# RWKV-6 attention with a SwiGLU layer: two of four batches of superblocks 2 and 3 get their normed x transposed by DMA

## Chip, cores and metric

The kernel runs on one core of one Trainium2 chip. The metric is the device time of one execution in microseconds (us). Its median before the change is 200.54 us, of 3 runs from 200.46 to 200.59.

## What is computed

The first part is an attention with a state (RWKV-6), over 4 batches, 8 heads, 768 time steps and a head size of 48. The second is a feed-forward layer (SwiGLU) over the 3072 rows that result, each 8 x 48 = 384 wide:

```
for t in range(S):                                  # each batch b, head h
    cur   = (u * k[t]) outer v[t]
    y[t]  = r[t] @ (state + cur)
    state = w[t][:, None] * state + k[t] outer v[t]

x  = y as (3072, 384)
xn = x / sqrt(mean(x*x) + 1e-6) * rms_g
out = (silu(xn @ w_gate) * (xn @ w_val)) @ w_out    # 384 -> 1536 -> 384
```

The change concerns the line of `xn`: x of a row divided by its root mean square, times the weights rms_g of the norm, and brought into the layout that the products with w_gate and w_val read.

## The kernel before

Time is cut into 6 superblocks (n) of 128 steps. Within one, each of the 4 batches (j) goes through the attention on its own, with 128 steps on the partitions and all 8 heads side by side (128x384). Then the feed-forward layer of the superblock runs over the 512 rows of its 4 batches at once: 12 blocks (f) of 128 columns of w_gate and w_val, and last the product with w_out, batch by batch.

All steps stand in one list, ORDER, as `function.n.j` (or `function.n.f`), and a loop at the end of the kernel calls them in that order. What an engine does is in the order of that list; an engine that waits holds back all that is behind it on that engine. SP issues nearly all DMAs from one queue, in order, and each waits there for its inputs and for an earlier transfer to have landed. The attention of superblock n+1 is mixed into the feed-forward steps of superblock n.

From the output y of a batch to the products, the steps are:

- `x_add` (L561, DVE), `x_sq` (L570, ACT) and `x_rstd` (L579 and L580, POOL) make x and one over its root mean square.
- `xn_mul` (L585, ACT) writes xn, 128x384 in bf16, still without rms_g.
- In superblocks 0 to 3, `xn_pe` (L596, PE) transposes it in three 128x128 pieces into a PSUM bank, and `xn_out` (L607, DVE) multiplies that by the weights gT, 128x384 at once, into the tile xnt (128 x 3 x 512: rms_g's index on the partitions, KC = 3 chunks of 128, and 128 columns for each batch).
- In superblocks 4 and 5, `xn_tr` (L590) lets a DMA transpose xn straight into xnt, and `xn_gain` (L615, on DVE, one chunk on ACT) multiplies xnt in place, a chunk of 128x512 for all four batches at a time.
- `gate_mm` and `val_mm` (L626, PE) read all 512 columns of xnt, so the first of a superblock waits for the last batch.

Other lines that are spoken of: L672 is `o_mm`, the product with w_out (PE). L425 is `cs_add`, L455 `r_mul`, L451 `w_tot`, L472 `bonus_sum` and L679 `o_out` (all DVE). L461 is `k_mul`, from superblock 2 on POOL, and L467 and L468 are the two products of `bonus_mul` (POOL), the second of which reads what the first wrote. L489 is `rk_tr`, the DMA transpose of r and k that `q_mm` (L502 and L504, PE) reads. L248 and L261 are the loads.

Of the kernel before, what the change touches and what calls it, by code (L numbers as in the profile page):

```python
# [74 lines left out]
exp_k.3.3 cs_mm.3.2 xn_out.2.3 o_mm.1.2 load_r.3.2 k_mul.3.1 w_tot.3.3 rk_tr.3.0 r_mul.3.3 cs_add.3.2 out_dma.1.0
xn_out.2.1 load_v.3.0 exp_r.3.2 gate_mm.2.5 exp_k.3.2 r_mul.3.2 w_tot.3.2 val_mm.2.0 gate_mm.2.0 bonus_mul.3.0
bonus_mul.3.2 k_mul.3.2 o_out.1.3 bonus_sum.3.0 silu.2.5 rk_tr.3.1 load_k.3.3 o_out.1.2 q_mm.3.0 silu.2.0 q_mask_e.3.0
val_mm.2.1 bonus_v.3.0 h_mul.2.0 gate_mm.2.1 load_w.4.1 load_v.3.1 load_k.4.3 st_mm.3.2 k_mul.3.3 q_copy_o.3.0
silu.2.1 rk_tr.3.2 load_v.4.0 rk_tr.3.3 val_mm.2.5 gate_mm.2.11 load_k.4.0 bonus_sum.3.1 cast_v.3.0 out_dma.1.1
load_v.3.3 load_w.5.2 q_mask_e.3.1 q_copy_o.3.1 gate_mm.2.2 silu.2.11 h_mul.2.5 val_mm.2.2 h_mul.2.1 load_w.4.0  # L80
gate_mm.2.3 load_v.4.1 silu.2.2 q_mask_o.3.0 cast_v.3.1 load_r.4.1 bonus_sum.3.2 h_mul.2.2 bonus_v.3.1 gate_mm.2.6
val_mm.2.3 y_mm.3.0 st_new.3.2 st_mm.3.0 silu.2.3 gate_mm.2.4 h_mul.2.3 silu.2.6 q_mask_o.3.1 st_new.3.0 st_mm.3.1
silu.2.4 x_add.3.0 load_k.4.1 gate_mm.2.7 val_mm.2.4 x_sq.3.0 gate_mm.2.10 out_dma.1.2 cast_v.4.0 st_new.3.1
val_mm.2.6 q_mm.3.2 h_mul.2.4 bonus_mul.3.3 h_mul.2.6 silu.2.7 val_mm.2.7 val_mm.2.10 load_w.4.3 x_rstd.3.0 silu.2.10
# [5 lines left out]
o_out.2.0 x_rstd.3.2 xn_mul.3.2 w_tot.4.0 ln.4.2 exp_r.4.1 load_r.5.1 x_rstd.3.3 k_mul.4.0 xn_out.3.0 load_r.4.3  # L90
out_dma.1.3 bonus_sum.4.1 xn_pe.3.1 xn_out.3.1 ln.4.3 exp_k.4.1 bonus_mul.4.2 xn_mul.3.3 r_mul.4.1 k_mul.4.1 w_tot.4.1
out_dma.2.0 o_mm.2.1 cs_mm.4.2 xn_pe.3.3 bonus_mul.4.0 cast_v.4.1 xn_pe.3.2 o_out.2.1 cs_mm.4.3 bonus_sum.4.2
rk_tr.4.0 xn_out.3.3 cs_add.4.3 load_k.5.3 o_mm.2.3 exp_r.4.3 xn_out.3.2 cs_add.4.2 bonus_mul.4.3 r_mul.4.3 w_tot.4.3
exp_k.4.3 exp_r.4.2 rk_tr.4.1 o_out.2.3 exp_k.4.2 load_v.4.2 val_mm.3.1 gate_mm.3.6 bonus_sum.4.0 k_mul.4.3 r_mul.4.2
st_mm.4.0 w_tot.4.2 load_r.5.3 load_k.5.0 val_mm.3.0 o_out.2.2 silu.3.6 st_new.4.0 k_mul.4.2 gate_mm.3.1 q_mm.4.0
cast_v.4.2 out_dma.2.2 bonus_sum.4.3 silu.3.1 gate_mm.3.0 q_copy_o.4.0 silu.3.0 h_mul.3.1 q_copy_o.4.1 gate_mm.3.3
val_mm.3.6 gate_mm.3.8 rk_tr.4.3 q_mask_e.4.0 h_mul.3.0 h_mul.3.6 st_mm.4.1 bonus_v.4.0 q_mask_e.4.1 q_mask_o.4.0
load_r.5.0 bonus_v.4.2 rk_tr.4.2 load_v.5.1 q_mask_o.4.1 bonus_v.4.1 silu.3.3 gate_mm.3.4 val_mm.3.4 val_mm.3.3
y_mm.4.0 silu.3.4 st_new.4.1 gate_mm.3.9 h_mul.3.4 load_v.4.3 load_r.5.2 load_k.5.1 silu.3.8 x_add.4.0 val_mm.3.8
gate_mm.3.2 q_mm.4.2 h_mul.3.3 h_mul.3.8 silu.3.9 val_mm.3.9 load_w.5.1 silu.3.2 gate_mm.3.10 q_mask_e.4.3  # L100
q_copy_o.4.3 y_mm.4.1 h_mul.3.9 bonus_mul.5.3 x_sq.4.0 q_mask_o.4.3 x_rstd.4.0 q_copy_o.4.2 bonus_v.4.3 silu.3.10
x_add.4.1 load_w.5.3 val_mm.3.10 gate_mm.3.7 q_mask_e.4.2 x_sq.4.1 bonus_sum.5.3 xn_mul.4.0 load_w.5.0 x_rstd.4.1
h_mul.3.10 silu.3.7 val_mm.3.2 gate_mm.3.5 h_mul.3.2 load_k.5.2 gate_mm.3.11 q_mask_o.4.2 y_mm.4.2 cast_v.4.3
xn_mul.4.1 val_mm.3.7 silu.3.5 bonus_mul.5.0 x_add.4.2 silu.3.11 ln.5.1 y_mm.4.3 h_mul.3.7 val_mm.3.11 x_add.4.3
load_v.5.3 x_sq.4.2 xn_tr.4.0 h_mul.3.11 x_sq.4.3 xn_tr.4.1 val_mm.3.5 st_mm.4.3 h_mul.3.5 x_rstd.4.2 cs_mm.5.1
cs_add.5.1 ln.5.2 xn_mul.4.2 x_rstd.4.3 o_mm.3.2 o_out.3.2 cs_mm.5.2 xn_tr.4.2 exp_k.5.1 cs_add.5.2 exp_r.5.1 o_mm.3.0
xn_mul.4.3 r_mul.5.1 ln.5.3 ln.5.0 xn_tr.4.3 cs_mm.5.0 st_new.4.3 exp_r.5.2 cast_v.5.3 exp_k.5.2 o_mm.3.1 out_dma.3.2
cs_add.5.0 out_dma.2.3 r_mul.5.2 exp_r.5.0 cs_mm.5.3 r_mul.5.0 st_mm.4.2 exp_k.5.0 cs_add.5.3 exp_r.5.3 o_mm.3.3
bonus_mul.5.1 xn_gain.4.0 xn_gain.4.2 xn_gain.4.1 k_mul.5.0 r_mul.5.3 exp_k.5.3 o_out.3.1 out_dma.2.1 o_out.3.0
gate_mm.4.0 val_mm.4.1 gate_mm.4.1 val_mm.4.0 bonus_sum.5.1 st_new.4.2 k_mul.5.1 k_mul.5.3 silu.4.0 load_v.5.0  # L110
rk_tr.5.0 silu.4.1 h_mul.4.0 gate_mm.4.3 gate_mm.4.2 rk_tr.5.1 silu.4.3 val_mm.4.2 bonus_sum.5.0 k_mul.5.2 gate_mm.4.4
silu.4.2 bonus_v.5.1 o_out.3.3 cast_v.5.0 h_mul.4.1 val_mm.4.3 q_mm.5.0 gate_mm.4.6 h_mul.4.2 bonus_mul.5.2 h_mul.4.3
silu.4.4 q_copy_o.5.0 q_mask_o.5.0 gate_mm.4.5 out_dma.3.1 q_mask_e.5.0 y_mm.5.0 silu.4.6 q_copy_o.5.1 bonus_v.5.0
rk_tr.5.2 load_v.5.2 silu.4.5 rk_tr.5.3 x_add.5.0 val_mm.4.4 q_mask_o.5.1 gate_mm.4.8 val_mm.4.5 q_mask_e.5.1
h_mul.4.4 bonus_sum.5.2 q_mm.5.2 q_copy_o.5.2 gate_mm.4.10 val_mm.4.6 bonus_v.5.3 cast_v.5.2 silu.4.8 h_mul.4.5
q_copy_o.5.3 cast_v.5.1 q_mask_e.5.3 q_mask_e.5.2 q_mask_o.5.2 silu.4.10 h_mul.4.6 gate_mm.4.7 x_sq.5.0 y_mm.5.1
q_mask_o.5.3 silu.4.7 bonus_v.5.2 x_rstd.5.0 x_add.5.1 val_mm.4.10 y_mm.5.3 val_mm.4.7 y_mm.5.2 gate_mm.4.11 x_add.5.3
x_sq.5.1 h_mul.4.10 x_sq.5.3 x_rstd.5.1 h_mul.4.7 xn_mul.5.1 val_mm.4.8 out_dma.3.3 gate_mm.4.9 silu.4.11 x_rstd.5.3
xn_mul.5.3 xn_tr.5.1 h_mul.4.8 xn_mul.5.0 val_mm.4.11 xn_tr.5.3 x_add.5.2 x_sq.5.2 x_rstd.5.2 val_mm.4.9 silu.4.9
h_mul.4.11 xn_mul.5.2 xn_tr.5.0 h_mul.4.9 xn_tr.5.2 xn_gain.5.1 xn_gain.5.0 o_mm.4.3 o_mm.4.0 o_mm.4.2 o_mm.4.1  # L120
o_out.4.1 xn_gain.5.2 gate_mm.5.2 gate_mm.5.1 val_mm.5.1 out_dma.4.1 val_mm.5.2 silu.5.1 silu.5.2 h_mul.5.2 h_mul.5.1
out_dma.3.0 gate_mm.5.5 o_out.4.0 gate_mm.5.0 val_mm.5.5 o_out.4.3 val_mm.5.0 silu.5.5 h_mul.5.5 o_out.4.2 out_dma.4.0
gate_mm.5.3 silu.5.0 gate_mm.5.7 out_dma.4.2 silu.5.3 h_mul.5.0 out_dma.4.3 val_mm.5.3 silu.5.7 h_mul.5.3 gate_mm.5.4
silu.5.4 gate_mm.5.8 val_mm.5.4 val_mm.5.7 gate_mm.5.9 silu.5.8 h_mul.5.4 gate_mm.5.6 h_mul.5.7 silu.5.6 val_mm.5.6
# [600 lines left out]
```

## Time and profile before

| | |
|---|---|
| median of 3 runs | 200.54 us |
| the profiled execution's own time | 200.28 us |
| its span | 198.6 us |
| granted clock of PE | 1.0 throughout |
| three transposes of one batch on PE (L596) | 0.33 us shown, four batches in each of superblocks 0 to 3 |
| product with the norm's weights from PSUM (L607) | 0.55 us, 16 times |
| the same in place, 128x512 (L615) | 0.50 us on average, 5 times on DVE |
| DMA transposes of xn (L590) | 8, 2.3 us to landing |
| DMA engines | busy over 90% in most of the first 150 us |

A row of the list in order of time reads: start, duration, engine, line, operation, what it writes <- what it reads, shapes, and how many are merged into the row; in brackets the time that the engine sat idle before it, and what ended that. A row of the waits reads: who waited, for whom, us in total, times, longest. Start times are from the beginning of the span. The steps before the products of superblock 2 lie between 81 and 90 us, those of superblock 3 between 105 and 118 us.

### The profile page before, as it was taken

The numbers are of one execution on the slowest core, as the hardware profiler recorded it, in microseconds if no ns is written. First come the engines' busy times: TensorE is split into PE (matmuls) and PEld (weight loads), VectorE is DVE, ScalarE is ACT, GpSimd is POOL, SyncE is SP. The second block draws the span as 40 slices with busy tenths as digits, with TensorE's granted clock in tenths as the row PEclk, the third lists the DMA queues.
The fourth block names the chain that finished last, engine by engine and source line by source line (L and its number), as shares of the span: only waits on it lengthen the run. The fifth ranks groups of instructions, "written<-read, shape, count | busy, mean of one in ns | idle before, by whom it ended". The sixth has DMA issues, their size and how long they took to land.

```text
span 198.6 us, 4409 instructions
## 1 busy us (share of the span) xinstructions
PE 191.9 (97%) x1577; PEld 113.9 (57%) x1577; DVE 151.4 (76%) x290; ACT 137.3 (69%) x279; POOL 125.2 (63%) x184
## 2 busy tenths in 40 slices
PE   7979998999999999999999999999999999999994
PEld 3556574465665565665556665556655565555562
DVE  6358989989998799987889989987887973173611
ACT  4399989579979569958559959399786683164300
POOL 5378993189399687899939899867686851000000
PEclk9999999999999999999999999999999999999999
DMA  6999999999999998999899879995499012032012
GB/s 153 268 235 176 183 220 203 214 180 211 179 195 224 206 196 196 236 198 207 193 195 225 188 171 204 204 183 107 138 187 208 0 25 60 6 112 83 0 59 101
DMA packets 121566, 32.41 MB, mean 163 GB/s; under 512 B 116420, under 2 KB 120392, under 8 KB 121544
## 3 DMA queue, kind: packets, MB, share of 16 engines
q1 hardware_dynamic: 119504, 28.58, 67.3%
q0 software_dynamic: 2032, 3.54, 10.0%
q8 instruction: 12, 0.20, 0.4%
q14 instruction: 10, 0.08, 0.1%
q10 hardware_dynamic: 8, 0.00, 0.0%
HBM read 25.96 MB, written 4.72 MB: 154 GB/s over the span
## 4 chain that ended last, share of the span: by engine, by line
PE 72%; SPq 18%; DMA 6%; POOL 2%; issue 1%; ACT 0%; POOLq 0%
SPq L248 16%; PE ps_av L626 10%; PE ps_bu L626 10%; PE ps_bv L626 10%; PE ps_au L626 10%; PE ps_qv L672 7%; PE ps_qz L672 7%; PE ps_qu L672 5%; PE ps_qx L672 4%; DMA wo_sb<-in_moe_w_out_dram 4%; DMA vt<-in_v_dram 3%; SPq L261 2%; PE ps_qz L502 1%; PE ps_qx L552 1%; PE ps_av L417 1%
## 5 line engine op out<-in xcount | busy, mean ns | idle before, releaser
L672 PEld LDWEIGHTS <-ht 128*128 128x128 bf16 x300 | 28.2, 98 | 17.0 <-issue 0.5
L626 PEld LDWEIGHTS <-wg_sb 128*128 128x128 bf16 x216 | 23.1, 114 | 19.7 <-DMA wg_sb<-in_moe_w_gate_dram 0.7
L626 PEld LDWEIGHTS <-wv_sb 128*128 128x128 bf16 x216 | 22.8, 114 | 19.0 <-DMA wv_sb<-in_moe_w_val_dram 1.0
L658 DVE TENSOR_TENSOR ht<-ps_bv,sg 128x512 bf16<-128x512 f32 x35 | 24.0, 686 | 10.1 <-PE ps_bv L626 9.2
L235 ACT ACTIVATE sg<-ps_av 128x512 bf16<-128x512 f32 x37 | 22.0, 595 | 12.3 <-PE ps_av L626 12.0
L626 PE MATMUL ps_av<-xnt,wg_sb 128*128 128x512 bf16 x111 | 30.1, 380 | 0.0
L626 PE MATMUL ps_bu<-xnt,wv_sb 128*128 128x512 bf16 x111 | 30.1, 380 | 0.0
L658 DVE TENSOR_TENSOR ht<-ps_bu,sg 128x512 bf16<-128x512 f32 x37 | 25.4, 686 | 6.0 <-PE ps_bu L626 5.2
L626 PE MATMUL ps_bv<-xnt,wv_sb 128*128 128x512 bf16 x105 | 28.5, 380 | 0.6 <-DMA wv_sb<-in_moe_w_val_dram 0.5
L626 PE MATMUL ps_au<-xnt,wg_sb 128*128 128x512 bf16 x105 | 28.5, 380 | 0.2 <-DMA wg_sb<-in_moe_w_gate_dram 0.2
L235 ACT ACTIVATE sg<-ps_au 128x512 bf16<-128x512 f32 x35 | 21.0, 599 | 10.8 <-PE ps_au L626 9.0
L467 POOL TENSOR_TENSOR ruk<-rt,kt 128x384 f32<-128x384 f32 x24 | 24.1, 1003 | 6.6 <-DMA kt<-in_k_dram 4.8
L468 POOL TENSOR_TENSOR ruk<-ruk,u_bc 128x384 f32<-128x384 f32 x24 | 24.4, 1017 | 1.9
L520 POOL TENSOR_SCALAR_AFFINE_SELECT qts<-qts 128x512 bf16<-128x512 bf16 x20 | 12.9, 653 | 15.1 <-ACT qts L513 14.6
L477 POOL TENSOR_TENSOR ydiag<-vt,diag 128x384 f32<-128x384 f32 x24 | 19.9, 833 | 1.0 <-DVE rk L461 0.5
L461 POOL TENSOR_TENSOR rk<-kt,ek 128x384 bf16<-128x384 f32 x16 | 15.9, 1007 | 2.3 <-ACT ek L235 2.3
L672 PE MATMUL ps_qv<-wo_sb,ht 128*128 128x384 bf16 (+1 forms) x96 | 15.0, 306 | 0.0
L672 PE MATMUL ps_qz<-wo_sb,ht 128*128 128x384 bf16 x84 | 14.8, 326 | 0.0
L233 ACT ACT_TABLE_LOAD x10 | 12.8, 1283 | 1.8 <-PEq L709 1.6
L235 ACT ACTIVATE lw<-wt 128x384 bf16<-128x384 f32 (+1 forms) x20 | 11.1, 578 | 4.2 <-DMA wt<-in_w_dram 4.1
L472 DVE TENSOR_REDUCE diag<-ruk 128x8 f32<-128x384 f32 x24 | 12.9, 543 | 0.7 <-POOL ruk L468 0.7
L585 ACT ACTIVATE xn<-xb,rstd 128x384 bf16<-128x384 f32 x20 | 11.8, 605 | 0.8 <-POOL rstd L580 0.8
(180 smaller groups left out, 373.6 us busy)
## 6 DMA issues: line engine op xcount, KB each, us to landing
rt<-in_r_dram SPq DMA_DIRECT2D x24, 192.0 KB, 3.9
kt<-in_k_dram SPq DMA_DIRECT2D x24, 192.0 KB, 4.0
vt<-in_v_dram SPq DMA_DIRECT2D x24, 192.0 KB, 3.7
out_dram<-ob SPq DMA_DIRECT2D x23, 192.0 KB, 2.3
wt<-in_w_dram SPq DMA_DIRECT2D x16, 192.0 KB, 4.0
wt<-in_w_dram SPq DMA_DIRECT2D x4, 384.0 KB, 4.4
wo_sb<-in_moe_w_out_dram POOLq DMA_DIRECT2D x3, 384.0 KB, 7.1
wg_sb<-in_moe_w_gate_dram POOLq DMA_DIRECT2D x1, 768.0 KB, 9.8
```

Of the source, the lines that this page charges most:

```text
L233: nc.scalar.preload_act_table_set(table_name)
L235: return nc.scalar.activation(**kw).ins
L248: dmas["load_" + which, n, j] = nc.sync.dma_start(out=inp[which, n, j], in_=t[j, :, n * L:(n + 1) * L, :].rearrange("h t d -> t h d")).ins
L461: eng.tensor_tensor(out=rk[:, n % 2, j, 1, :, 0:D], in0=inp["k", n, j], in1=bank["cs_k", n, j][:, 0:DM].rearrange("p (h d) -> p h d", h=H) ...
L467: nc.gpsimd.tensor_tensor(out=ruk[n, j], in0=inp["r", n, j], in1=inp["k", n, j], op=ALU.mult)
L468: nc.gpsimd.tensor_tensor(out=ruk[n, j], in0=ruk[n, j], in1=u_bc, op=ALU.mult)
L472: nc.vector.tensor_reduce(out=diag[n, j].rearrange("p h o -> p (h o)"), in_=ruk[n, j], axis=mybir.AxisListType.X, op=ALU.add)
L477: nc.gpsimd.tensor_tensor(out=ydiag[n, j], in0=inp["v", n, j], in1=diag[n, j].to_broadcast([128, H, D]), op=ALU.mult)
L520: nc.gpsimd.affine_select(out=qts[n, j][:, 1], in_=qts[n, j][:, 1], compare_op=ALU.is_gt, fill=0.0, base=0, pattern=[[0, NP], [1, 128]], c ...
L626: nc.tensor.matmul(ps[:, cols], lhsT=units(ws, c, f), rhs=xnt[n][:, c, cols], start=(first and c == 0), stop=(c == KC - 1))
L658: nc.vector.tensor_tensor(out=ht[n][:, f, :], in0=bank.pop(("v", n, f)), in1=bank.pop(("sg", n, f)), op=ALU.mult)
L672: nc.tensor.matmul(ps[:, cols], lhsT=ht[n][:, f, b * L:(b + 1) * L], rhs=wo_sb[:, f, cols], start=(f == 0), stop=(f == FC - 1))
```

## The change

For batches 0 and 1 of superblocks 2 and 3, the three transposes on PE (`xn_pe`) leave the list, and a DMA transpose into xnt (`xn_tr`, SP's queue) comes in at an earlier or later place. `xn_out` for them then multiplies xnt in place, SBUF to SBUF, in three DVE instructions of 128x128. Batches 2 and 3 stay as they were.

```diff
@@ ORDER (the other lines move only by the wrapping) @@
-load_r.3.0 x_sq.2.2 xn_mul.2.0 cast_v.3.2 cs_add.3.0 x_add.2.3 exp_k.3.0 x_sq.2.3 o_mm.1.0 cs_mm.3.1 xn_pe.2.0
+load_r.3.0 x_sq.2.2 xn_mul.2.0 cast_v.3.2 cs_add.3.0 x_add.2.3 exp_k.3.0 x_sq.2.3 o_mm.1.0 cs_mm.3.1 exp_r.3.0 ln.3.2
...
+xn_pe.2.3 o_out.1.1 cs_add.3.3 r_mul.3.1 load_k.3.2 xn_tr.2.0 load_r.3.3 xn_out.2.0 exp_r.3.3 exp_k.3.3 cs_mm.3.2
+xn_out.2.3 o_mm.1.2 load_r.3.2 xn_tr.2.1 k_mul.3.1 w_tot.3.3 rk_tr.3.0 r_mul.3.3 cs_add.3.2 out_dma.1.0 xn_out.2.1
...
@@ -192,6 +192,7 @@
     X_PE = sel("00 01 02 03")
     EARLY = 13
+    XT_DMA = sel("30 20 31 21")
     OUT_DVE = sel("00 02 10 12 20 22 30 32 40 42 50 52 53")
@@ -598,6 +599,11 @@
     def xn_out(n, j):
         if n not in xnt:
             xnt[n] = pt.tile([128, KC, TS], BF16, name="xnt")
+        if (n, j) in XT_DMA:
+            for c in range(KC):
+                t = xnt[n][:, c, j * L:(j + 1) * L]
+                nc.vector.tensor_scalar(out=t, in0=t, scalar1=gT[:, c:c + 1], scalar2=None, op0=ALU.mult)
+            return
         ps = bank.pop(("xt", n, j))
         if (n, j) in XOUT_ACT:
```

DVE's own list just before the products of superblock 2, before the change: the products for batches 2, 0, 3 and 1, in this order, are the four rows that write xnt.

```order
L607 TENSOR_TENSOR xnt<-ps_qv,gT 128x3x128
L451 TENSOR_TENSOR wcol<-ps_av,half_of 128x8
L425 TENSOR_TENSOR ps_bu<-ps_au,lw 128x384
L455 TENSOR_TENSOR rk<-rt,ps_av 128x8x48
L607 TENSOR_TENSOR xnt<-ps_qx,gT 128x3x128
L607 TENSOR_TENSOR xnt<-ps_qv,gT 128x3x128
L451 TENSOR_TENSOR wcol<-ps_au,half_of 128x8
L455 TENSOR_TENSOR rk<-rt,ps_au 128x8x48
L425 TENSOR_TENSOR ps_bv<-ps_av,lw 128x384
L607 TENSOR_TENSOR xnt<-ps_qu,gT 128x3x128
```

The same place on DVE in the changed kernel, whose line numbers are 1 higher behind L194 and 6 higher behind L601:

```order
L613 TENSOR_TENSOR xnt<-ps_qu,gT 128x3x128
L452 TENSOR_TENSOR wcol<-ps_av,half_of 128x8
L426 TENSOR_TENSOR ps_bu<-ps_au,lw 128x384
L456 TENSOR_TENSOR rk<-rt,ps_av 128x8x48
L605 TENSOR_SCALAR xnt<-xnt,gT 128x128 x3
L613 TENSOR_TENSOR xnt<-ps_qz,gT 128x3x128
L452 TENSOR_TENSOR wcol<-ps_au,half_of 128x8
L456 TENSOR_TENSOR rk<-rt,ps_au 128x8x48
L426 TENSOR_TENSOR ps_bv<-ps_av,lw 128x384
L605 TENSOR_SCALAR xnt<-xnt,gT 128x128 x3
```

Nothing has moved: in place of the products of batches 0 and 1 there stand three instructions each, which read SBUF and not PSUM; the banks of the others have other names.

SP's list at the same place, before the change, from the load of k of superblock 3, batch 2 on:

```order
L248 DMA kt<-in_k_dram 128x8x48
L248 DMA rt<-in_r_dram 128x8x48 x2
L489 DMA_TRANSPOSE rkT<-rk 128x8x128
L687 DMA out_dram<-ob 128x384
L248 DMA vt<-in_v_dram 128x8x48
L489 DMA_TRANSPOSE rkT<-rk 128x8x128
```

And in the changed kernel:

```order
L249 DMA kt<-in_k_dram 128x8x48
L591 DMA_TRANSPOSE xnt<-xn 128x3x128
L249 DMA rt<-in_r_dram 128x8x48 x2
L591 DMA_TRANSPOSE xnt<-xn 128x3x128
L490 DMA_TRANSPOSE rkT<-rk 128x8x128
L693 DMA out_dram<-ob 128x384
L249 DMA vt<-in_v_dram 128x8x48
L490 DMA_TRANSPOSE rkT<-rk 128x8x128
```

Batch 0's transpose now stands ahead of two loads of r, and batch 1's between them and the transposes of r and k for superblock 3.

SP's list before the products of superblock 3, before the change:

```order
L261 DMA wt<-in_w_dram 128x8x48
L248 DMA rt<-in_r_dram 128x8x48 x2
L261 DMA wt<-in_w_dram 128x8x48
L248 DMA kt<-in_k_dram 128x8x48
L248 DMA rt<-in_r_dram 128x8x48 x2
L687 DMA out_dram<-ob 128x384 x2
L489 DMA_TRANSPOSE rkT<-rk 128x8x128
```

And in the changed kernel:

```order
L262 DMA wt<-in_w_dram 128x8x48
L249 DMA rt<-in_r_dram 128x8x48
L591 DMA_TRANSPOSE xnt<-xn 128x3x128
L249 DMA rt<-in_r_dram 128x8x48
L262 DMA wt<-in_w_dram 128x8x48
L249 DMA kt<-in_k_dram 128x8x48
L249 DMA rt<-in_r_dram 128x8x48
L591 DMA_TRANSPOSE xnt<-xn 128x3x128
L249 DMA rt<-in_r_dram 128x8x48
L693 DMA out_dram<-ob 128x384 x2
L490 DMA_TRANSPOSE rkT<-rk 128x8x128
```

Here each of the two transposes stands between two loads of r.

More of the change, by code (lines that the diff above doesn't have):

```diff
@@ L75 @@
[L75 to L84, printed above, removed]
@@ L90 @@
[L90 to L99, printed above, removed]
@@ L100 @@
[L100 to L124, printed above, removed]
@@ new lines @@
+q_mask_o.5.0 gate_mm.4.5 out_dma.3.1 q_mask_e.5.0 y_mm.5.0 silu.4.6 q_copy_o.5.1 bonus_v.5.0 rk_tr.5.2 load_v.5.2
+silu.4.5 rk_tr.5.3 x_add.5.0 val_mm.4.4 q_mask_o.5.1 gate_mm.4.8 val_mm.4.5 q_mask_e.5.1 h_mul.4.4 bonus_sum.5.2
+q_mm.5.2 q_copy_o.5.2 gate_mm.4.10 val_mm.4.6 bonus_v.5.3 cast_v.5.2 silu.4.8 h_mul.4.5 q_copy_o.5.3 cast_v.5.1
+q_mask_e.5.3 q_mask_e.5.2 q_mask_o.5.2 silu.4.10 h_mul.4.6 gate_mm.4.7 x_sq.5.0 y_mm.5.1 q_mask_o.5.3 silu.4.7
+bonus_v.5.2 x_rstd.5.0 x_add.5.1 val_mm.4.10 y_mm.5.3 val_mm.4.7 y_mm.5.2 gate_mm.4.11 x_add.5.3 x_sq.5.1 h_mul.4.10
```

58 lines of the change are left out of this document (48 added, 10 removed).

## The prediction

> **What bounds the kernel now.** I read the page's busy shares first, then who PE waits for, then the order of time around the two places that change.
>
> ```profile
> span 198.6 us, 4409 instructions
> PE 191.9 (97%) x1577; PEld 113.9 (57%) x1577; DVE 151.4 (76%) x290; ACT 137.3 (69%) x279; POOL 125.2 (63%) x184
> PE ps_qx L672 <- DMA wo_sb<-in_moe_w_out_dram: 0.3, 1, 0.3
> ```
>
> The third line is the whole answer for PE as the waiter between 53 and 198 us: one wait of 0.3 us. Past 53 us PE's own work is the path. So what the change takes from PE is gained in full, and every wait that it puts before PE is lost in full: no slack behind it takes it back. The stretch before the products of superblock 2, all engines, in order of time:
>
> ```profile
> 82.66 0.33 PE L596 MATMUL ps_qx<-ident,xn 128*128 128x128 bf16 x3
> 82.83 2.11 PE L672 MATMUL ps_qu<-wo_sb,ht 128*128 128x384 bf16 x12
> ...
> 86.15 1.00 POOL L461 TENSOR_TENSOR rk<-kt,ek 128x384 bf16<-128x384 f32 x1
> ...
> 86.62 0.55 DVE L607 TENSOR_TENSOR xnt<-ps_qx,gT 128x384 bf16<-128x384 bf16 x1
> ...
> 87.11 1.00 POOL L467 TENSOR_TENSOR ruk<-rt,kt 128x384 f32<-128x384 f32 x1
> ...
> 87.52 0.56 DVE L607 TENSOR_TENSOR xnt<-ps_qv,gT 128x384 bf16<-128x384 bf16 x1 [0.36 <-PE ps_qv L596]
> ...
> 88.19 0.99 POOL L468 TENSOR_TENSOR ruk<-ruk,u_bc 128x384 f32<-128x384 f32 x1
> ...
> 89.00 0.55 DVE L607 TENSOR_TENSOR xnt<-ps_qu,gT 128x384 bf16<-128x384 bf16 x1
> ...
> 89.14 1.00 POOL L467 TENSOR_TENSOR ruk<-rt,kt 128x384 f32<-128x384 f32 x1
> ...
> 89.70 0.81 PE L626 MATMUL ps_au<-xnt,wg_sb 128*128 128x512 bf16 x3
> ...
> 90.22 1.01 POOL L468 TENSOR_TENSOR ruk<-ruk,u_bc 128x384 f32<-128x384 f32 x1
> ```
>
> Two things are to be seen. The last product with the norm's weights (batch 1, DVE, 89.00 + 0.55) ends at 89.55, and the first gate product, which reads all four batches, starts at 89.70: **DVE is 0.15 us ahead of PE here.** And POOL runs op behind op, about 1.0 us each, through the whole stretch.
>
> **Removed.** Twelve transposes on PE. Three of them push the next matmul back by 82.83 - 82.66 = 0.17 us, though each shows 0.22 us of duration: they overlap. Four groups give 4 x 0.165 = 0.66 us, 0.33 per superblock. The Trainium skill (TensorE: Matmul & The Clock Gate, Part 4: PE-mode transpose) has about 275 ns for one such transpose inside a kernel; by that the saving would be an estimated 12 x 0.275 = 3.3 us, but the starts here are 0.055 us apart, and the sum goes by the 0.66.
>
> Also removed are four DVE products of 0.55 us that read PSUM, and four uses of a PSUM bank; the other users of that ring only get freer.
>
> **Added on DVE.** Three products of 128x128 in place, SBUF to SBUF, for each batch. The trace has this operation as 128x512 in superblocks 4 and 5 (L615), once with POOL idle and once with POOL busy:
>
> ```profile
> 168.44 0.88 DVE L615 TENSOR_SCALAR xnt<-xnt,gT 128x512 bf16<-128x512 bf16 x3 [2.82 <-DMA xnt<-xn]
> ...
> 144.42 1.35 DVE L615 TENSOR_SCALAR xnt<-xnt,gT 128x512 bf16<-128x512 bf16 x2
> ...
> 144.52 1.10 POOL L461 TENSOR_TENSOR rk<-kt,ek 128x384 bf16<-128x384 f32 x1
> ...
> L615 DVE TENSOR_SCALAR xnt<-xnt,gT x2: 346/718/1090, 144.4 to 144.7; 128x512 bf16<-128x512 bf16 x2
> ...
> 23.16 1.06 DVE L461 TENSOR_TENSOR rk<-kt,ek 128x384 bf16<-128x384 f32 x1
> 24.15 1.35 DVE L455 TENSOR_TENSOR rk<-rt,er 128x384 bf16<-128x384 f32 x1
> ...
> 22.81 0.99 POOL L467 TENSOR_TENSOR ruk<-rt,kt 128x384 f32<-128x384 f32 x1
> 23.88 1.20 POOL L468 TENSOR_TENSOR ruk<-ruk,u_bc 128x384 f32<-128x384 f32 x1
> ```
>
> Alone, three take 0.88 us: about 0.34 each, a start every 0.27. At a quarter of the columns an estimate from this row is 0.2 us and a start every 0.12 to 0.17, so 0.45 to 0.6 us for three, as much as the 0.55 removed. **With POOL busy the second one took 1.09 us**: it ends at 144.42 + 1.35 = 145.77, just behind POOL's op (144.52 + 1.10 = 145.62). The rows at 23 to 25 us say the same of other DVE work from SBUF: 23.16 + 1.06 = 24.22 is 0.42 us after POOL's 22.81 + 0.99 = 23.80, and 24.15 + 1.35 = 25.50 is 0.42 us after 23.88 + 1.20 = 25.08. Each waited out the POOL op in front of it, and POOL's 1.20 in place of 1.00 shows it waiting in turn. The products that go away read PSUM and show 0.55 us whatever POOL does.
>
> The Trainium skill (SBUF — State Buffer, Who interferes with whom) speaks against the change: a DVE tensor_scalar in SBUF can run in a mode with two ports, and then it and a GpSimd op exclude one another, the earlier one for its whole length. The trace agrees (1.09 beside 0.35 us); no row shows the form of 128 columns.
>
> Now the sum for superblock 2, in times of this profile. PE's group for batch 2 comes 0.17 us earlier, and so does DVE up to the product of batch 0: start 86.45. Its first third waits for POOL's L461 (ends 87.15) and ends at 87.2. POOL's next op starts before that one ends (87.11), so the second third waits for L467 and ends at 88.15. Between L467 and L468, which needs L467's result, POOL leaves 0.08 us (88.11 to 88.19); I take it that the last third slips in there, 88.3. That is 1.1 us later than 86.62 + 0.55 = 87.17. Behind it on DVE stand batch 3's product, a short L451, L455 and L425: from 87.52 to 89.00 they took 1.48 us, so batch 1's thirds start near 89.75. The first waits for L467 (now about 90.15), the second slips in at 90.35, the third waits for L468 and ends at 91.25. The gate product starts at 91.3 in place of 89.70: **+1.6 us**, the 0.33 saved on PE being swallowed. ACT, POOL and the products behind it start that much later together, so nothing else comes due.
>
> Superblock 3:
>
> ```profile
> 112.96 0.55 DVE L607 TENSOR_TENSOR xnt<-ps_qx,gT 128x384 bf16<-128x384 bf16 x1
> ...
> 113.09 1.00 POOL L467 TENSOR_TENSOR ruk<-rt,kt 128x384 f32<-128x384 f32 x1
> 114.17 1.00 POOL L468 TENSOR_TENSOR ruk<-ruk,u_bc 128x384 f32<-128x384 f32 x1
> 115.12 1.00 POOL L461 TENSOR_TENSOR rk<-kt,ek 128x384 bf16<-128x384 f32 x1
> 116.09 0.99 POOL L467 TENSOR_TENSOR ruk<-rt,kt 128x384 f32<-128x384 f32 x1
> ...
> 116.13 0.56 DVE L607 TENSOR_TENSOR xnt<-ps_qx,gT 128x384 bf16<-128x384 bf16 x1 [0.38 <-PE ps_qx L596]
> ...
> 117.09 0.55 DVE L607 TENSOR_TENSOR xnt<-ps_qu,gT 128x384 bf16<-128x384 bf16 x1
> ...
> 118.31 0.59 PE L626 MATMUL ps_bv<-xnt,wv_sb 128*128 128x512 bf16 x2
> ```
>
> Here DVE ends at 117.64, 0.67 us ahead of PE. Batch 0's thirds start at 112.95 and by the same count end at 113.2, 114.1 and 114.3; batch 1's, behind two reductions and L455, start at 115.7 and end at 116.15, 117.1 and 117.3. The products of batches 3 and 2 follow to 118.75, and the first product of the superblock starts at 118.8 in place of 118.31: **+0.5 us**.
>
> **Added on SP.** Four DMA transposes on the one queue, the second of each pair behind loads. The eight that are there now:
>
> ```profile
> L590 SPq DMA_TRANSPOSE xnt<-xn x8: 1178/1198/1390, 133.5 to 166.0; - x8
> ...
> DMA to landing us min/median/max: 2.3/2.3/3.1
> ...
> 81.19 0.60 ACT L585 ACTIVATE xn<-xb,rstd 128x384 bf16<-128x384 f32 x1
> ...
> 83.90 1.36 SPq L489 DMA_TRANSPOSE rkT<-rk  x1
> ...
> 87.18 1.24 SPq L489 DMA_TRANSPOSE rkT<-rk  x1
> ...
> 111.50 1.10 ACT L585 ACTIVATE xn<-xb,rstd 128x384 bf16<-128x384 f32 x2
> ...
> 113.46 1.34 SPq L489 DMA_TRANSPOSE rkT<-rk  x1
> ```
>
> Each holds the queue 1.2 us and waits at its head for its x. Batch 0's x is ready at 81.8, so its transpose lands by 81.85 + 3.1 = 84.95, well before 86.45; batch 1's is issued near 84.2 and lands by 87.3, before 89.75. The two transposes of r and k move from 83.90 to 85.5 and from 87.18 to 87.85; at 2.8 us to landing the later one is there at 90.65, and PE's first reader started at 91.74: 1.1 us of cover. In superblock 3 the second transpose waits for x until 112.05 and pushes one load of r, two outputs and the r,k transpose of 113.46 back to about 115. The load of r lands near 117.2 and is read at 118. I cost all of SP at nothing, the cover being 0.8 to 1.1 us.
>
> **Sum.** 200.28 us (profiled execution) + 1.6 + 0.5 = 202.4. The median before is 0.26 above that execution, so **202.6**.
>
> **Bounds and rivals.**
>
> Upper end: no third slips into a seam, each waits for a POOL op of its own. In superblock 2 batch 0 then ends at 89.3, a POOL op later, batch 1 near 92.6, and the gate product is 3 us late; superblock 3, one op for each batch, 2 us: 200.28 + 5 = 205.3, with the offset 205.5. For it: the second op at 144.42 did just that. Against: 0.08 us gaps inside each pair L467, L468. Chance 0.18.
>
> **The other side: no lock at 128 columns.** A third of a quarter of the length might run in DVE's single-port way, or be done before POOL's next request, as the first op at 144.42 was (0.35 us beside a busy POOL). Then three take 0.45 to 0.6, DVE keeps its 0.15 us lead, and the whole 0.66 is gained: 199.6, as a median 199.9. It decides at 0.85 us for three: then DVE ends at 89.55 - 0.17 + 2 x (0.85 - 0.55) = 89.98 and the gate product is 0.33 us late, which is what superblock 3 gains; above that the change loses. Chance 0.15. By the skill's 275 ns per transpose this case would give 197; the 0.055 us between starts leave that 0.02.
>
> **The queue decides, not DVE.** If each added transpose costs SP 2 us more than its issue (waits for earlier transfers while the DMA rows are full), the r,k transpose lands near 93.7 and PE waits 2 us for it, another 1 us in superblock 3, or DVE sits waiting for xnt as the 2.82 us at 168.44 show that it can. The change would then not free PE at all: 200.28 - 0.66 + 3 = 202.6 without any lock. Chance 0.07.
>
> **Even.** Locks of a few tenths that the 0.66 pays for: within 0.4 us of before. Chance 0.08.
>
> **Chances.** The forecast has the remaining 0.50, with its own range 201.2 to 204.2. Slower by over 0.2% (0.4 us, about what a measurement can tell from no change): 0.50 + 0.18 + 0.07 = 0.75; faster 0.17; within 0.08. The range runs from the no-lock case, 199.8, to the upper end, 205.5.
>
> **What would show it.** Right: DVE shows 12 products of 128x128 with a mean near 0.6 us or more, most ending just behind a POOL op; PE waiting for DVE's xnt before the first product of superblocks 2 (most) and 3; POOL ops of 1.1 to 1.2 us there. Wrong: a mean near 0.2 us with no PE wait (then faster), or PE waiting at q_mm for rkT (then it is the queue), or DVE waiting for the transpose's landing.

## The result, and the profile after

| | before | after |
|---|---|---|
| median of 4 runs each | 200.50 us (200.18 to 200.59) | 203.90 us (203.65 to 204.13) |
| profiled execution | 200.28 us, span 198.6 | 203.77 us, span 202.1 |

The ratio is 1.0171, with a 95% interval of 1.0141 to 1.0200: the change costs 3.4 us. The forecast was 202.6 within 199.8 to 205.5, so the sign and the range held, and the loss was 1.3 us larger than the 2.1 predicted. Medians and ratios, here and below, leave out the few slow executions, which took over 1.5% longer than the fastest of the same kernel.

The page of the changed kernel:

```profile
span 202.1 us, 4380 instructions
PE 193.0 (96%) x1545; PEld 113.9 (56%) x1565; DVE 154.4 (76%) x298; ACT 137.3 (68%) x279; POOL 125.2 (62%) x184
```

And all that PE waits for between 53 and 198 us (who waits, for what, us in total, times, longest):

```profile
PE ps_bv L632 <- DVE ps_bu L426: 1.4, 1, 1.4
PE ps_au L632 <- DVE xnt L605: 1.1, 2, 0.7
```

Before, there was one wait of 0.3 us here. Now there are two places, and only one of them names the thirds (L605). The other names the add L426, which the change doesn't touch.

To see what each place costs, I cut the span at four instructions of PE that every kernel here has. In the trace of before they start at these times:

```profile
80.45 2.11 PE L672 MATMUL ps_qz<-wo_sb,ht 128*128 128x384 bf16 x12
...
91.74 0.23 PE L502 MATMUL ps_qv<-rkT 48*128 48x128 bf16 x1
...
109.48 0.33 PE L672 MATMUL ps_qv<-wo_sb,ht 128*128 128x384 bf16 x1
...
137.41 0.33 PE L672 MATMUL ps_qu<-wo_sb,ht 128*128 128x384 bf16 x1
```

The first lies ahead of superblock 2's changed places, the second behind its first products, the third ahead of nearly all of superblock 3's changed places (one group of three transposes of PE stands just before it), the fourth past superblock 3's first products and past the matmuls on r and k (L502 in before, L503 after) that follow them. Differences to before, in us, each from one profiled execution:

| kernel | up to 1st | superblock 2 | between | superblock 3 | rest | sum of the three in the middle |
|---|---|---|---|---|---|---|
| before (its own times) | 80.45 | 11.29 | 17.74 | 27.93 | 61.19 | 56.96 |
| after | +0.66 | +1.16 | -0.17 | +1.35 | +0.50 | +2.34 |

So 2.34 us arise where the kernel was changed. The 0.66 us up to the first cut are there before any changed instruction runs, and profiled executions of the kernels below, which have the same order up to there, are between -0.51 and +2.38 us. One execution of each kernel can't tell whether the change has a part in it. Of the 0.50 us at the end, 0.3 lie behind PE's last matmul, which starts 3.2 us later than before; no cause was found for them.

**Superblock 2 after, in order of time** (the thirds one by one, between POOL's operations):

```profile
86.79 0.99 POOL L462 TENSOR_TENSOR rk<-kt,ek 128x384 bf16<-128x384 f32 x1
87.11 0.73 DVE L605 TENSOR_SCALAR xnt<-xnt,gT 128x128 bf16<-128x128 bf16 x1
87.75 1.00 POOL L468 TENSOR_TENSOR ruk<-rt,kt 128x384 f32<-128x384 f32 x1
87.76 1.04 DVE L605 TENSOR_SCALAR xnt<-xnt,gT 128x128 bf16<-128x128 bf16 x1
88.82 1.00 POOL L469 TENSOR_TENSOR ruk<-ruk,u_bc 128x384 f32<-128x384 f32 x1
...
89.78 1.00 POOL L468 TENSOR_TENSOR ruk<-rt,kt 128x384 f32<-128x384 f32 x1
90.35 0.47 DVE L605 TENSOR_SCALAR xnt<-xnt,gT 128x128 bf16<-128x128 bf16 x1
90.85 1.00 POOL L469 TENSOR_TENSOR ruk<-ruk,u_bc 128x384 f32<-128x384 f32 x1
90.88 0.62 PE L632 MATMUL ps_au<-xnt,wg_sb 128*128 128x512 bf16 x2 [0.69 <-DVE xnt L605]
90.90 1.00 DVE L605 TENSOR_SCALAR xnt<-xnt,gT 128x128 bf16<-128x128 bf16 x1
91.95 0.38 PE L632 MATMUL ps_au<-xnt,wg_sb 128*128 128x512 bf16 x1 [0.45 <-DVE xnt L605]
```

Four thirds end 0.04 to 0.06 us behind a POOL operation: 87.84 behind 87.78, 88.80 behind 88.75, 90.82 behind 90.78, 91.90 behind 91.85. The other two slip into gaps between POOL's operations (they are not in the list: the third of batch 0 runs from 88.72 to 88.96, the second of batch 1 from 90.74 to 90.98). And PE waits twice. The first product is three matmuls, one for each chunk of 128 of rms_g's index, and a third is just such a chunk. So each matmul waits only for its own third: the first two start from 90.88 on, the last at 91.95.

**Superblock 3.** First a chain of before that the prediction didn't follow. The first product of this superblock goes into bank ps_bv, and these two rows are what frees it:

```profile
116.61 0.57 DVE L425 TENSOR_TENSOR ps_bv<-ps_av,lw 128x384 f32<-128x384 f32 x1
...
117.60 0.48 ACT L235 ACTIVATE ek<-ps_bv 128x384 f32<-128x384 f32 x1
```

DVE adds into ps_bv, ACT takes two exponentials, and the second one reads ps_bv until 118.08. PE's product started at 118.31: **0.23 us of slack**, while xnt itself had 0.67. The same place after:

```profile
114.78 0.57 DVE L605 TENSOR_SCALAR xnt<-xnt,gT 128x128 bf16<-128x128 bf16 x3
...
115.21 1.00 POOL L468 TENSOR_TENSOR ruk<-rt,kt 128x384 f32<-128x384 f32 x1 [0.28 <-DMA kt<-in_k_dram]
...
117.32 0.55 DVE L473 TENSOR_REDUCE diag<-ruk 128x8 f32<-128x384 f32 x1 [0.98 <-POOL ruk L469]
117.79 1.62 DVE L605 TENSOR_SCALAR xnt<-xnt,gT 128x128 bf16<-128x128 bf16 x3
...
119.81 0.55 DVE L426 TENSOR_TENSOR ps_bv<-ps_av,lw 128x384 f32<-128x384 f32 x1
...
120.78 0.49 ACT L236 ACTIVATE ek<-ps_bv 128x384 f32<-128x384 f32 x1
...
121.31 0.81 PE L632 MATMUL ps_bv<-xnt,wv_sb 128*128 128x512 bf16 x2 [1.36 <-DVE ps_bu L426]
```

The first three thirds met a POOL that waited 0.28 us for k, and took 0.57 us together. The next three took 1.62, the add stands behind them, the bank is free at 121.27, and PE starts 0.04 us later. The wait's name (L426) is of the last event only; the path goes through ACT's row, which is the one that has to be done with ps_bv.

The change also moved a product here. In before, the product of batch 1 stands behind the first of two reductions, and DVE waits for POOL and then for PE before it comes to the add:

```profile
113.89 0.55 DVE L607 TENSOR_TENSOR xnt<-ps_qu,gT 128x384 bf16<-128x384 bf16 x1
...
115.20 0.55 DVE L472 TENSOR_REDUCE diag<-ruk 128x8 f32<-128x384 f32 x1 [0.23 <-POOL ruk L468]
```

In the changed kernel, batch 1's thirds stand behind the second reduction and have only batch 3's product between them and the add. The prediction counted them there; it is this place that lets them hold up the bank. By the triple that took 0.57 us, an estimate of the lock's share of the 1.62 is 1.05 us. Of PE's 1.36 us that leaves about 0.3 for the new place and for POOL's late k together. No run has the thirds at this place without the lock.

And the load of k, on SP's queue, before and after:

```profile
107.35 1.05 SPq L248 DMA_DIRECT2D kt<-in_k_dram  x1
```

```profile
108.32 1.72 SPq L591 DMA_TRANSPOSE xnt<-xn  x1
...
111.33 0.75 SPq L249 DMA_DIRECT2D kt<-in_k_dram  x1
```

It is issued 4.0 us later, though PE at the third cut is only 1.65 us later. So SP was not free of cost.

### The profile page after: what moved, and what is told of

It is laid out like the page before. It is cut to its first block, busy times and chain, and to the rows that moved or that the text cites. A ratio compares the mean times of both kernels' runs of the same rounds, so it can differ in the third digit from the quotient of the medians.

```text
span 202.1 us, 4380 instructions
## 1 busy us (share of the span) xinstructions
PE 193.0 (96%) x1545; PEld 113.9 (56%) x1565; DVE 154.4 (76%) x298; ACT 137.3 (68%) x279; POOL 125.2 (62%) x184
## 3 DMA queue, kind: packets, MB, share of 16 engines
q1 hardware_dynamic: 121168, 28.98, 68.5%
## 4 chain that ended last, share of the span: by engine, by line
PE 74%; DVE 8%; SPq 7%; DMA 4%; issue 3%; POOL 1%; ACT 0%; DVEq 0%; POOLq 0%
PE ps_av L632 11%; PE ps_bu L632 11%; PE ps_bv L632 10%; PE ps_au L632 10%; PE ps_qx L678 5%; PE ps_qz L678 5%; DMA kt<-in_k_dram 4%; SPq L249 4%; PE ps_qu L678 4%; PE ps_qv L678 4%; SPq L262 2%; DVE xnt L605 2%; DVE rk L456 1%; PE ps_qx L503 1%; DVE diag L473 1%
## 5 line engine op out<-in xcount | busy, mean ns | idle before, releaser
L632 PE MATMUL ps_bu<-xnt,wv_sb 128*128 128x512 bf16 x101 | 29.2, 380 | 0.6
L632 PE MATMUL ps_bv<-xnt,wv_sb 128*128 128x512 bf16 x100 | 28.0, 380 | 1.7 <-DVE ps_bu L426 1.4
L586 ACT ACTIVATE xn<-xb,rstd 128x384 bf16<-128x384 f32 x20 | 11.8, 604 | 1.8 <-POOL ruk L469 1.0
L678 PE MATMUL ps_qu<-wo_sb,ht 128*128 128x384 bf16 x72 | 12.8, 326 | 0.0
```

Source lines behind the costliest of these rows:

```text
L586: nc.scalar.activation(out=xn, in_=xb[n, j], func=AF.Copy, scale=rstd[n, j][:, 1, c:c + 1])
L632: nc.tensor.matmul(ps[:, cols], lhsT=units(ws, c, f), rhs=xnt[n][:, c, cols], start=(first and c == 0), stop=(c == KC - 1))
L678: nc.tensor.matmul(ps[:, cols], lhsT=ht[n][:, f, b * L:(b + 1) * L], rhs=wo_sb[:, f, cols], start=(f == 0), stop=(f == FC - 1))
```

## The experiments

All go by the same cuts. Times are medians; "before" on the same chip had medians of 200.68, 200.50 and 200.44 us for the three groups of runs (the first four kernels, the next four, the last four).

| kernel | median us | ratio to before (95%) | up to 1st | superblock 2 | between | superblock 3 | sum of three |
|---|---|---|---|---|---|---|---|
| thirds on ACT | 203.13 | 1.0119 (1.0073 to 1.0165) | +0.27 | -0.33 | +0.26 | +1.35 | +1.28 |
| no products | 201.73 | 1.0061 (1.0030 to 1.0092) | +0.73 | -0.33 | 0.00 | +1.67 | +1.34 |
| thirds from PSUM | 200.97 | 1.0022 (0.9997 to 1.0046) | +0.36 | +0.01 | 0.00 | -0.01 | 0.00 |
| one product in place | 202.76 | 1.0112 (1.0047 to 1.0177) | +0.61 | +0.29 | -0.16 | +1.22 | +1.35 |
| superblock 2 alone | 202.50 | 1.0110 (1.0072 to 1.0149) | +2.38 | +1.17 | 0.00 | 0.00 | +1.17 |
| superblock 3 alone | 202.57 | 1.0098 (1.0064 to 1.0131) | +0.36 | 0.00 | -0.16 | +1.09 | +0.93 |
| no products, moved | 202.10 | 1.0082 (1.0050 to 1.0113) | +1.05 | -0.33 | -0.16 | +1.97 | +1.48 |
| ACT, moved | 201.86 | 1.0076 (1.0039 to 1.0112) | +1.51 | +0.32 | +0.24 | +0.40 | +0.96 |
| 3 alone, no products | 201.77 | 1.0077 (1.0048 to 1.0106) | +0.72 | 0.00 | -0.16 | +0.92 | +0.76 |
| 3 alone, late thirds | 203.18 | 1.0132 (1.0090 to 1.0173) | -0.51 | 0.00 | -0.16 | +1.50 | +1.34 |
| 2 alone, ACT | 201.80 | 1.0079 (1.0048 to 1.0111) | +1.64 | -0.18 | +0.42 | -0.01 | +0.23 |
| 3 alone, ACT | 201.63 | 1.0058 (1.0031 to 1.0085) | +1.40 | 0.00 | -0.16 | +0.05 | -0.11 |

The sums leave something out. Each is of one execution, and some of these stand at the edge of their kernel's times (thirds on ACT and late thirds are the fastest of theirs, superblock 2 alone is the slowest). Set against the medians, the kernels with added transposes are between 0.3 us less and 1.4 us more over before than their sum of three: thirds on ACT 2.45 against 1.28, superblock 3 alone with ACT 1.19 against -0.11. For the changed kernel it is 3.40 against 2.34. About a microsecond of what most of them lose is thus not explained by the changed places. Some medians by themselves point elsewhere than the cuts: those of thirds on ACT and of superblock 2 alone lie where the expectations below put a late queue, and that of superblock 3 alone lies above both of its. What follows rests on the cuts and on the rows.

The theory was that the products in place wait out POOL's operations (the lock); the rival, that SP's queue is late (the queue).

**Thirds on ACT.** The DMA transposes stay, DVE gets nothing in place of the products.

```diff
-                nc.vector.tensor_scalar(out=t, in0=t, scalar1=gT[:, c:c + 1], scalar2=None, op0=ALU.mult)
+                nc.scalar.activation(out=t, in_=t, func=AF.Copy, scale=gT[:, c:c + 1])
```

> The twelve products in place go from DVE to ACT, everything else as in the changed kernel. If DVE waiting out POOL's operations is what costs (theory of the lock), the stall before the first product of superblocks 2 and 3 goes, less what ACT loses by six products of about 0.3 us each ahead of its exponentials: 200 to 201.2 us. If SP's longer queue (late loads, late transposes) is what costs, nothing changes: 203 us or more.

**No products.** The three lines of the loop are gone, so x of these four batches stays without the norm's weights.

> The products with the norm's weights are left out for the four batches that a DMA transposes; the transposes stay in SP's queue. Theory of the lock: no DVE work in place, so nothing waits for POOL, and the PE time of the twelve transposes is won: 199.6 to 200.2 us. Theory of the queue: the late loads and transposes are all still there: 203 us or more. In between: both take part.

Superblock 2 is the same in both: -0.33 us, just the two groups of transposes that PE no longer does. With DVE out of it the whole loss there is gone, so the lock is its cause. Superblock 3 went the other way: more loss than in the changed kernel, without any product on DVE. The trace of the run without products:

```profile
109.44 1.01 POOL L468 TENSOR_TENSOR ruk<-rt,kt 128x384 f32<-128x384 f32 x1 [1.75 <-DMA kt<-in_k_dram]
```

```profile
116.66 0.34 PE L597 MATMUL ps_qz<-ident,xn 128*128 128x128 bf16 x3 [0.53 <-ACT xn L586]
120.25 0.81 PE L629 MATMUL ps_bv<-xnt,wv_sb 128*128 128x512 bf16 x2 [0.87 <-DVE ps_bu L426]
```

POOL waits 1.75 us for k, then does the norm's rows late, ACT gets them late, and PE waits for x. So there are two delays in superblock 3, and either alone costs over a microsecond. In the changed kernel POOL's longest wait for k is 0.52 us: superblock 2's stall, 1.5 us against these two runs, may have given the loads that time. That is argued, not shown. With the thirds on ACT the loss of superblock 3 is one wait of PE for x from ACT (L586), 1.36 us. POOL waits 1.17 us for k ahead of it, and ACT has the additional work; this run doesn't separate the two.

**Thirds from PSUM.** The kernel before, with DVE's product of these four batches cut in three instructions that read PSUM; nothing goes by DMA.

```diff
+        if (n, j) in THIRDS:
+            for c in range(KC):
+                nc.vector.tensor_scalar(out=xnt[n][:, c, j * L:(j + 1) * L], in0=ps[:, c, :], scalar1=gT[:, c:c + 1],
+                                        scalar2=None, op0=ALU.mult)
+            return
```

> The kernel before with its transposes on PE; only the product of these four batches is cut into three instructions of 128x128 that read PSUM. If the cost is three instructions in place of one (more DVE time), this shows it: 201.5 us or more. Theory of the lock: reading PSUM they do not meet POOL, and three of about 0.25 us take little more than one of 0.55: 200.3 to 200.9 us, within 0.2% of before.

```profile
86.98 0.66 DVE L605 TENSOR_SCALAR xnt<-ps_qx,gT 128x128 bf16<-128x128 bf16 x3
89.36 0.66 DVE L605 TENSOR_SCALAR xnt<-ps_qu,gT 128x128 bf16<-128x128 bf16 x3
113.33 0.66 DVE L605 TENSOR_SCALAR xnt<-ps_qx,gT 128x128 bf16<-128x128 bf16 x3
114.36 0.66 DVE L605 TENSOR_SCALAR xnt<-ps_qu,gT 128x128 bf16<-128x128 bf16 x3
```

Three instructions take 0.66 us wherever they stand, in the same stretch of POOL work in which three in place took 0.57 to 1.85. The cuts agree with before to 0.01 us. Cutting in three costs nothing; in superblock 2, where the thirds stand at the same place of DVE's list as in the change, it is the operand in SBUF. In superblock 3 batch 1's thirds have the old place here, so this run says nothing of the new one.

**One product in place.** One tensor_tensor of 128x384 in place for each batch.

```diff
-            for c in range(KC):
-                t = xnt[n][:, c, j * L:(j + 1) * L]
-                nc.vector.tensor_scalar(out=t, in0=t, scalar1=gT[:, c:c + 1], scalar2=None, op0=ALU.mult)
+            t = xnt[n][:, :, j * L:(j + 1) * L]
+            nc.vector.tensor_tensor(out=t, in0=t, in1=gT.to_broadcast([128, KC, L]), op=ALU.mult)
```

> The changed kernel with one product of 128x384 in place per batch (two inputs in SBUF) in place of three of 128x128. Theory of the lock: one wait for a POOL operation per batch and not two, then 0.42 us: about 1.0 to 1.4 us per batch against 1.6 to 1.85, so 201.5 to 203.3 us. If the number of waits does not matter but only that the work reads SBUF: 203.9 us as changed.

```profile
L604 DVE TENSOR_TENSOR xnt<-xnt,gT x4: 839/912/1100, 87.1 to 117.5; 128x384 bf16<-128x384 bf16 x4
```

One operation meets at most one POOL operation: 0.84 to 1.10 us each (minimum, median, maximum in ns) where the product from PSUM took 0.55, and superblock 2 loses 0.29 in place of 1.16. Superblock 3 still loses 1.22, though batch 1's product takes only 0.87 us there: POOL waits 0.64 us for k, and the reduction ahead of the product waits 1.33 us for POOL. So 0.64 us of that is the queue's. The Trainium skill (SBUF — State Buffer, Who interferes with whom) says that a DVE operation with two inputs in SBUF contends with POOL's reads, that whoever comes first keeps the shared ports for the whole instruction, and that ACT and PE wait for nobody. The runs agree: 0.84 us and more here, thirds that end 0.05 us behind POOL's operations after, and no stall in superblock 2 in the run with the thirds on ACT.

**Superblock 2 alone** and **superblock 3 alone.** The set of batches is cut in two; the other superblock keeps its transposes on PE and the order of before.

```diff
-    XT_DMA = sel("30 20 31 21")
+    XT_DMA = sel("20 21")
```

> Only batches 0 and 1 of superblock 2 go by DMA and by thirds; superblock 3 is as before. Both theories expect superblock 2's +1.16 us again (first gate product late behind the thirds). Theory of a carried delay (SP's queue, once late from superblock 2's transposes, is still late in superblock 3, so that its loads of k and r come late there too): part of superblock 3's +1.3 us appears though nothing was changed there, and the time is 1.7 to 2.5 us over before. Theory of superblock 3's own transposes (they wait for x at the head of SP's queue, with the load of k behind them): superblock 3 takes its 11.69 us as before, and the time is 0.8 to 1.4 us over before.

> Only batches 0 and 1 of superblock 3 go by DMA and by thirds; superblock 2 is as before. Theory of superblock 3's own transposes: its first product is again 1.2 to 1.4 us late, behind the late load of k, and the time is 1.0 to 1.6 us over before. Theory of a carried delay: without superblock 2's two transposes the load of k is less late, the stall there falls to 0.5 us or less (what the lock alone was computed to cost), and the time is 0 to 0.7 us over before.

Superblock 2 alone loses 1.17 us and superblock 3 comes out as before; superblock 3 alone loses 0.93 net. By the cuts the losses add up: 2.10 of the 2.34. By the medians they are 2.0 and 2.1 us, together more than the 3.4 of the change. Here is superblock 3 alone:

```profile
113.32 1.39 DVE L605 TENSOR_SCALAR xnt<-xnt,gT 128x128 bf16<-128x128 bf16 x3
...
116.09 1.62 DVE L605 TENSOR_SCALAR xnt<-xnt,gT 128x128 bf16<-128x128 bf16 x3
...
118.09 0.55 DVE L426 TENSOR_TENSOR ps_bv<-ps_av,lw 128x384 f32<-128x384 f32 x1
...
119.61 0.81 PE L632 MATMUL ps_bv<-xnt,wv_sb 128*128 128x512 bf16 x3 [1.10 <-DVE ps_bu L426]
```

POOL does not wait for k here, and both triples meet the lock. The stall of 1.10 us stands behind the add. I had expected the cause to be the late load of k; this run, and the one below that also leaves the products out, say that it was the lock, at the place where the change put batch 1's thirds.

**No products, moved** and **ACT, moved.** Three of the four DMA transposes are issued later in the order, so that fewer loads stand behind a transpose that waits for x; the first of the two leaves the products out.

```diff
-load_k.3.2 xn_tr.2.0 load_r.3.3
+load_k.3.2 load_r.3.3 xn_tr.2.0
...
-xn_mul.3.0 xn_tr.3.0
+load_k.4.2 xn_tr.3.0
...
-load_r.5.1 xn_tr.3.1
+out_dma.1.3 xn_tr.3.1
```

> The weights' product is left out for the four batches (as in the run before of that kind), and three of the four DMA transposes are issued later in SP's order: superblock 2's first behind a load of r, superblock 3's first behind the load of k, its second behind a load of r and an output. The same DMA work, less waiting at the head of the queue. Theory of the queue's order (loads stand behind a transpose that waits for x): superblock 3's wait of 1.5 us goes, both superblocks come 0.33 us earlier, and the time is 0.3 to 0.7 us below before. Theory of the DMA engines' time (a transpose takes 1.2 us of all 16 engines, so loads come late wherever it stands): the stall stays within 0.4 us of what it was, and the time is 0.7 to 1.3 us over before.

> The thirds on ACT instead of DVE, and the three transposes moved as in the kernel beside it. If the lock (DVE) and the queue's order are the two causes, both are gone: superblock 2 at -0.33 us, superblock 3 between -0.33 and +0.3 (ACT has twelve operations more), the time 0.3 to 0.7 us below before or equal to it. If the DMA engines' time is the cause in superblock 3, or ACT's twelve operations come due there, it is 0.7 to 1.5 us over before.

Neither came out as the theory of the queue's order had it. Without products the loss in superblock 3 stayed:

```profile
119.89 0.81 PE L629 MATMUL ps_bv<-xnt,wv_sb 128*128 128x512 bf16 x3 [1.03 <-DVE wcol L452]
123.92 0.23 PE L503 MATMUL ps_qx<-rkT 48*128 48x128 bf16 x1 [0.78 <-DMA rkT<-rk]
```

POOL still waited 1.1 us for k, and now PE waits for the transposed r and k too. The next load of k did go out earlier (110.28 in place of 111.70), but the time didn't come back. With the thirds on ACT the loss of superblock 3 fell from 1.35 to 0.40 us. But superblock 2 now lost 0.32 (ACT waits 1.32 us for a DMA transpose there), and PE was 1.51 us late at the first cut in place of 0.27, which leaves loads more time; whether the new order or the later PE did it stays open. What may speak for the amount of DMA work is the share that the engines are busy, here of before (the last but one number):

```profile
80.00:100.00 20.00, 20.00 (x163) 12.06 (x162) 17.45 (x37) 14.92 (x32) 18.33 (x25) 1.00 0.99 208
100.00:120.00 20.00, 20.00 (x181) 12.28 (x180) 18.62 (x40) 15.73 (x35) 15.84 (x24) 1.00 0.91 196
...
140.00:160.00 20.00, 20.00 (x163) 11.55 (x161) 16.69 (x31) 14.72 (x30) 15.05 (x21) 1.00 0.61 133
```

The changed places of superblocks 2 and 3 lie where the 16 engines are busy for 0.99 and 0.91 of the time; the kernel's older DMA transposes, of superblocks 4 and 5, run from 133 us on, mostly where the share is lower. No run varies the amount of DMA work by itself.

**Superblock 3 alone, no products**, and **superblock 3 alone, late thirds.** The second moves batch 1's products on DVE behind the second add.

```diff
-bonus_sum.4.2 xn_out.3.1 rk_tr.4.0
+bonus_sum.4.2 rk_tr.4.0
...
-xn_out.3.2 cs_add.4.2 bonus_mul.4.3
+xn_out.3.2 cs_add.4.2 xn_out.3.1 bonus_mul.4.3
```

> Only batches 0 and 1 of superblock 3 go by DMA, and their product with the weights is left out. Theory of lock and bank (in the run with superblock 3 alone, DVE's two triples hold back the add L426 into bank ps_bv, and with it the two exponentials that free it for the first product): the stall of 1.1 us goes altogether, superblock 3 takes 11.3 to 11.4 us between its anchors in place of 11.69, the time is 0 to 0.5 us below before. Theory of the queue (the added transposes make the load of k and the work behind it late): a stall of 0.7 us or more stays, the time is 0.5 to 1.5 us over before.

> Superblock 3 alone, on DVE by thirds as in the change, but batch 1's three products stand on DVE behind the second add (L426) and no longer ahead of the first. Theory of the bank: the add into ps_bv comes at its old place (about 7.1 us behind the start of o_mm.2.0), the bank is free in time, and PE waits for the late thirds themselves (named xnt), 0.2 to 0.7 us in all in place of 1.1. If the first product waits by the thirds' own length wherever they stand: 1.0 us or more as before.

Without products the stall before the first product is gone, and another one has come up behind it:

```profile
118.69 0.81 PE L629 MATMUL ps_bv<-xnt,wv_sb 128*128 128x512 bf16 x2
...
122.87 0.23 PE L503 MATMUL ps_qv<-rkT 48*128 48x128 bf16 x1 [0.92 <-DMA rkT<-rk]
```

118.69 is 8.65 us behind the third cut; in before it was 8.83, so PE has its 0.18 us. The first stall is there only with the products at that place, as lock and bank have it. But the two r,k transposes that follow on SP, pushed back behind the added one, now land 0.92 us too late. With the products, in superblock 3 alone, PE has no such wait: the stall before it covers it.

With the late thirds:

```profile
117.76 0.82 PE L632 MATMUL ps_bv<-xnt,wv_sb 128*128 128x512 bf16 x2
119.16 0.38 PE L632 MATMUL ps_bv<-xnt,wv_sb 128*128 128x512 bf16 x1 [0.58 <-DVE xnt L605]
119.70 0.41 PE L632 MATMUL ps_av<-xnt,wg_sb 128*128 128x512 bf16 x1 [0.17 <-DVE wcol L452]
```

The first product starts 8.95 us behind the third cut: the bank was free, as the theory of the bank has it. The gain of 0.4 us or more that I expected did not come, since the three thirds took 1.93 us there and the last one held PE up. At both places PE waits for something behind them, and superblock 3 lost more with the late thirds, 1.50 us in place of 1.09.

**Superblock 2 alone, ACT**, and **superblock 3 alone, ACT.** Each superblock by itself with the thirds on ACT.

> Superblock 2 alone, its thirds on ACT, so no lock. Theory of an uncovered delay (superblock 2's two transposes make the loads behind them 2 to 4 us late on full DMA engines; a stall of PE in superblock 2 gives that time back, without it POOL waits for k in superblock 3): superblock 2 at -0.33 us, superblock 3 at +0.8 to +1.5 us though nothing was changed there, the time 0.4 to 1.2 us over before. Theory that the lock was all: superblock 2 at -0.33, superblock 3 as before (11.69), the time 0.2 to 0.4 us below before.

> Superblock 3 alone, its thirds on ACT, so no lock, and no transposes in superblock 2 where the DMA engines are full. If both causes are out of the way: superblock 3 between -0.33 and +0.2 us (ACT has six operations of 0.3 us more ahead of the exponentials), the time from 0.4 us below before to even with it. If the queue's delay comes from superblock 3's own transposes, or ACT's six operations come due: 0.5 to 1.3 us over before.

Superblock 2 alone loses 0.42 us between the second and the third cut, 0.24 of it in a wait of PE for transposed r and k, and nothing in superblock 3, where I had expected 0.8 to 1.5. But POOL waits 0.70 us for k there, and in the runs with superblock 3 alone 0.28 us at most. So the late load of k comes in part from superblock 2's transposes; by themselves they made it less late than in the run without products (1.75), and PE didn't feel it in superblock 3. Superblock 3 alone with ACT is the only run with a gain in the changed places, 0.11 us, and still its median is 1.2 us over before. One thing may join the two: this execution was 1.40 us late at the first cut, and a late PE leaves loads more time, as superblock 2's stall may have done. An execution that starts sooner would then wait for r and k as the run without products does. That is argued, not shown. No version here beats the kernel before.

## Why the prediction was right in its sign and off in its size

- **PE's saving, 0.33 us per superblock:** right. Superblock 2 shows -0.33 without products, superblock 3 -0.16 and -0.18 on either side of the third cut.
- **The lock at 128 columns:** right. The triples of superblock 2 were computed as 86.45 to 88.3 and 89.75 to 91.25, 1.85 and 1.5 us. They took 1.85 and, from 90.35 to 91.90, 1.55, with the same two thirds in the gaps. Measured from the first cut the last third ends at 10.79 us, and 10.80 was predicted. Two details of the list of signs were wrong: POOL's operations stayed at 1.00 us, and the mean third is 0.52 us and not 0.6 or more, because the first three of superblock 3 came while POOL waited for k, and others slipped into gaps.
- **Superblock 2, +1.6 us:** too much by 0.44. DVE was right to 0.01 us, but I let the whole product wait for the last third. PE's first two matmuls, some 0.43 us of work, need only the first two.
- **Superblock 3, +0.5 us:** this step failed. With PE's saving counted in, it was 1.35 - 0.17 = 1.18 us. "The first product of the superblock starts at 118.8" took xnt for what PE waits for. It waits for a bank, and by the prediction's own times the chain would have given it: the thirds and batch 3's product end near 117.8, so the add moves from 116.61 to 117.8, and behind 0.23 us of slack that is 0.96 us. Superblock 3 alone measured 1.09; the changed kernel's further 0.26 is about the 0.28 us that POOL waits for k there.
- **"I cost all of SP at nothing":** wrong as a statement, small in the sum. The load of k is 4.0 us late in place of the push of about 1.5 us that I gave the r,k transpose, and costs POOL 0.28 us in the changed kernel. Its price shows when the lock is taken away: 1.3 us in the three stretches with all four batches. The rival of the queue was right that SP can cost this much without any lock, and too large: +2.3 us with PE's saving counted in, against 1.3. It looked for the waits at the r,k transposes; without products PE waited 1.40 us in superblock 3 behind the late load of k, and nowhere for the r,k transposes.
- The two wrong terms nearly cancel, 1.6 + 0.5 = 2.1 against 1.16 - 0.17 + 1.35 = 2.34, and that is luck: one was too large by 0.44, the other too small by 0.68. The other 1.16 us of the profiled execution's 3.5 are 0.66 before the first cut and 0.50 behind the last. The runs don't settle how much of these belongs to the change; the kernel with thirds from PSUM, which adds no DMA, has +0.36 and about +0.2.

## What to carry to other kernels

Before a wait is priced, list everything that the waiting instruction needs, its output bank too, with the slack of each: the operand with the longest slack may be the one that you moved, and the one with the shortest may hang on the same engine by another path. See too whether work that moves on an engine comes to stand closer to what others wait for. When work moves to DMA, look at the loads that stand behind it on the same queue: the issue time of the same transfer elsewhere, 1.2 us, did not foretell a load that went out 4.0 us later. And a stall can hide a second one: take away the first alone and see whether the time comes back, before you credit it with the whole loss.
